# A delta-rule attention with its feed-forward on one core: the feed-forward of one chunk placed between the pieces of the next chunk's units, and two vector operations fewer in the conversion of a weight part

## The chip, the cores and the metric

The kernel runs on one core of a Trainium2 chip. The metric is the device time of one execution in microseconds (us). A core has five engines that each execute their own queue in order: TensorE (PE; its weight loads are shown apart as PEld), VectorE (DVE), ScalarE (ACT), GpSimd (POOL) and SyncE (SP), which here only issues DMAs. ScalarE issues DMAs too (the weights). Matmul results go to PSUM; everything else is in SBUF or, for two small re-layouts, in DRAM.

## The reference

For 4 batches x 8 heads, a sequence of 768 steps with a state of 48 x 48 per head, and then a feed-forward layer over all 3072 tokens with 384 features and 2048 hidden ones:

```python
k_n = k / (np.linalg.norm(k, axis=-1, keepdims=True) + 1e-06)
for t in range(S):
    y[:, :, t] = np.einsum('bhd,bhde->bhe', q[:, :, t], state)
    v_old = np.einsum('bhde,bhd->bhe', state, kt)
    state = state + bt[:, :, :, None] * np.einsum('bhd,bhe->bhde', kt, vt - v_old)
...
x = y.transpose(0, 2, 1, 3).reshape(B * S, H * D)
h = x @ w_in
g = h * (1.0 / (1.0 + np.exp(-1.702 * h)))
return (g @ w_out).astype(np.float32)
```

q, k, v and beta are fp32. The two weight matrices are fp64 and are turned into fp32 on the chip.

## The kernel before, in words

The sequence is cut into 6 chunks of 128 steps (`NC`). Within a chunk the recurrence is solved in closed form: with N the strictly lower part of beta k k^T, the updates U follow from the inverse of (1 + N), and the state is only read and written once a chunk. A *unit* is one batch in one chunk, with its 8 heads; there are 24 units.

- **Loads.** `load(n)` (lines 80 to 88) issues K, Q and V of a unit on SyncE. K has 3 buffers, V 6, Q two zero-padded tiles `QP`. Two units are loaded ahead.
- **Preparation.** `prepare(n)` (172 to 231): GpSimd and VectorE compute 1/|k| (`ksq`, `ssq`, `rn`) and the scaled `KN`; PE transposes K and Q (`psT`, line 193), ScalarE copies them to `kqT`; PE forms k k^T and k q^T (`psG`, line 205); VectorE turns the first into `Nn` (line 210), ScalarE the second into `M` (line 214), which GpSimd masks (line 216). The 32 x 32 diagonal blocks of `Nn` go through DRAM (`Nd`, four DMAs) into `NT`, where one partition holds one block of all units of the chunk.
- **Inversion.** `invert(c)` (234 to 291) inverts these 128 blocks together on VectorE: 15 steps of a product and a sum (lines 259 and 263), then eight pairs of larger ones (242 and 243), with one copy on ScalarE (267). The products `P` use the tag `gT`. The result `YB` goes back through DRAM (`Yb`), one DMA for each batch.
- **Assembly.** `assemble(n)` (294 to 359) builds the inverse of the 128 x 128 matrix from its diagonal blocks: DMAs bring the blocks into `XT` (line 304, three buffers) and `XO` (311, two buffers); then a chain of four groups of products with something between each: `ps1` (325), a copy to `P1` on VectorE (327), `ps2` (330), four activations into `XT` (335), `ps3` (349), a copy to `P3` (353), `ps4` (356), an activation (359). `L32`, `XE` and `XA` have one buffer each.
- **Step.** `advance(n, xT)` (362 to 416): `psK` (369) and two VectorE operations on V, `psU` (377), its copy `U` (381), `psS` for the state (386), `psY` (394 and 399), `x` on ScalarE (404), the state's update (409), transposes `psXT` (415) and their copy into `xT` (416), which collects two batches.
- **Feed-forward.** `feed_forward(c, b0, xT)` (419 to 444) handles two batches of a chunk: 48 products into `ph` (428), a gelu for every second hidden block into `gT` (432, tag `gT` with 5 buffers, four of which hold one half of the feed-forward), then 32 products into `po` (438), a copy and a store. A chunk has two such halves.
- **Weights.** `load_weights(part)` (151 to 165), 28 parts: a DMA on ScalarE's queue brings the fp64 words (`raw`, tag `gT`), and `from_double` (122 to 145) makes fp32 of them with seven VectorE operations.

The order: `prepare_chunk(0)` with the inversion, then for each chunk: assemble and advance its four units, in chunk 0 load the weights, prepare the next chunk and invert it, and then the chunk's feed-forward (lines 446 to 468). The program is written in this order, and a scheduler that runs when the kernel is built sets the order on each engine from it: an operation that stands earlier in the program goes first, and a later one takes its place where it is expected to be ready while the earlier ones are not. Each engine then executes its queue in that fixed order. Buffers of one tag are handed out in the order of the program.

## Time and profile before

| | before |
|---|---|
| median of 3 runs | 1281.66 us (1278.46 to 1283.55) |
| the profiled execution's own time | 1283.35 us |
| its span, first to last instruction | 1281.6 us |
| mean granted clock of TensorE | 0.768 |
| busy, PE / PEld | 1024.0 / 837.8 us |
| busy, DVE / ACT / POOL | 438.9 / 203.5 / 117.0 us |
| mean DMA rate | 36 GB/s, 46.54 MB |

A row of a view names the line of the kernel, the engine, the operation and what it writes and reads (buffer numbers left out), then busy time and mean time, or start and time taken. The trace records an fp32 product as two matmuls (48 first products of a half of the feed-forward appear as x96), a transpose as one. "<-" names what ended the idle time ahead of an instruction. "PEclk" is the clock granted to TensorE, 1.00 or 0.50 here in any one moment, and a mean over the stretch where a stretch is shown.

### The profile page before, as it was taken

The numbers are of one execution on the slowest core, as the hardware profiler recorded it, in microseconds if no ns is written. First come the engines' busy times: TensorE is split into PE (matmuls) and PEld (weight loads), VectorE is DVE, ScalarE is ACT, GpSimd is POOL, SyncE is SP. The second block draws the span as 40 slices with busy tenths as digits, with TensorE's granted clock in tenths as the row PEclk, the third lists the DMA queues.
The fourth block names the chain that finished last, engine by engine and source line by source line (L and its number), as shares of the span: only waits on it lengthen the run. The fifth ranks groups of instructions, "written<-read, shape, count | busy, mean of one in ns | idle before, by whom it ended". The sixth has DMA issues, their size and how long they took to land. (4 is left out here: it accounts for less than half of the span.)

```text
span 1281.6 us, 12617 instructions
## 1 busy us (share of the span) xinstructions
PE 1024.0 (80%) x4974; PEld 837.8 (65%) x4974; DVE 438.9 (34%) x1020; ACT 203.5 (16%) x488; POOL 117.0 (9%) x112
## 2 busy tenths in 40 slices
PE   2408971199999299999389999479999669999998
PEld 1308951077798177698267699357699457699875
DVE  4395489910233620133530132540132460022000
ACT  1202121011112111111311111311111310111100
POOL 7300013000012100022100021100010100000000
PEclk9855665599758689857789857779956879955799
DMA  6233155010102210011210011210010210000000
GB/s 101 58 110 76 47 147 139 25 39 7 33 14 39 44 40 7 19 27 31 52 33 13 16 30 29 55 34 12 15 19 1 46 33 13 15 7 1 1 13 13
DMA packets 150827, 46.54 MB, mean 36 GB/s; under 512 B 142544, under 2 KB 145616, under 8 KB 150768
## 3 DMA queue, kind: packets, MB, share of 16 engines
q1 hardware_dynamic: 146688, 33.06, 13.0%
q10 hardware_dynamic: 4080, 12.68, 3.2%
q8 instruction: 39, 0.64, 0.2%
q14 instruction: 20, 0.16, 0.0%
HBM read 34.70 MB, written 11.01 MB: 36 GB/s over the span
## 5 line engine op out<-in xcount | busy, mean ns | idle before, releaser
L428 PE MATMUL ph<-xT,w_in 128*128 128x256 f32 x1152 | 284.6, 406 | 142.6 <-ACT gT L432 142.6
L428 PEld LDWEIGHTS ph<-xT,w_in 128*128 128x128 f32 x1152 | 230.9, 205 | 178.5 <-ACT gT L432 144.9
L438 PE MATMUL po<-w_out,gT 128*128 128x384 f32 x768 | 249.6, 486 | 0.0
L438 PEld LDWEIGHTS po<-w_out,gT 128*128 128x128 f32 x768 | 145.9, 190 | 99.2
L443 DVE COPY o<-po 128x384 f32<-128x384 f32 x24 | 13.4, 557 | 413.2 <-PE po L438 413.2
L432 ACT ACTIVATE gT<-ph 128x512 f32<-128x512 f32 x96 | 56.8, 597 | 335.6 <-PE ph L428 310.3
L186 POOL TENSOR_TENSOR KN<-K,rn 128x384 f32<-128x384 f32 x24 | 20.0, 834 | 732.0 <-PE psS L386 727.4
L377 PEld LDWEIGHTS psU<-V,XT 128*128 128x128 f32 x384 | 77.2, 304 | 1.6
L377 PE MATMUL psU<-V,XT 128*128 128x48 f32 x384 | 78.0, 383 | 0.0
L325 PE MATMUL ps<-XO,L 128*128 128x32 f32 x192 | 41.2, 375 | 42.1 <-DMA XO<-Yb 42.1
L205 PE MATMUL psG<-kqT 48*128 48x256 f32 x384 | 62.9, 458 | 10.2 <-ACT kqT L194 8.0
L325 PEld LDWEIGHTS ps<-XO,L 128*128 128x128 f32 x192 | 39.1, 299 | 45.9 <-issue 42.5
L399 PE MATMUL psY<-U,M 128*128 128x48 f32 x384 | 68.9, 352 | 0.0
L399 PEld LDWEIGHTS psY<-U,M 128*128 128x128 f32 x384 | 68.3, 274 | 0.2
L205 PEld LDWEIGHTS psG<-kqT 48*128 48x128 f32 x384 | 42.9, 221 | 23.1 <-ACT kqT L194 13.3
L319 ACT ACTIVATE L<-Nn 32x128 f32<-32x128 f32 x96 | 29.5, 307 | 146.3 <-PE ps L325 144.7
L349 PE MATMUL ps<-XT,Nn 64*64 64x64 f32 x384 | 45.1, 293 | 5.6 <-ACT XT L335 5.6
L210 DVE TENSOR_TENSOR Nn<-psG,betaT 128x256 f32<-128x256 f32 x96 | 36.8, 417 | 33.5 <-PE psG L205 31.2
L356 PEld LDWEIGHTS ps<-P,XA 64*64 64x64 f32 x384 | 38.9, 202 | 13.8 <-DVE P L353 6.5
L356 PE MATMUL ps<-P,XA 64*64 64x64 f32 x384 | 43.6, 295 | 5.4 <-DVE P L353 5.4
L193 PE MATMUL psT<-ident,KN 128*128 128x128 f32 x96 | 18.5, 325 | 35.9 <-POOL KN L186 23.1
L214 ACT ACTIVATE M<-psG 128x256 f32<-128x256 f32 x96 | 34.4, 381 | 77.7 <-DVE Nn L210 68.0
(72 smaller groups left out, 983.4 us busy)
## 6 DMA issues: line engine op xcount, KB each, us to landing
raw<-in_moe_w_in_dram ACTq DMA_DIRECT2D x12, 512.0 KB, 4.4
raw<-in_moe_w_out_dram ACTq DMA_DIRECT2D x16, 384.0 KB, 3.1
K<-in_k_dram SPq DMA_DIRECT2D x24, 192.0 KB, 2.7
V<-in_v_dram SPq DMA_DIRECT2D x24, 192.0 KB, 2.8
QP<-in_q_dram SPq DMA_DIRECT2D x24, 192.0 KB, 3.1
out_dram<-o SPq DMA_DIRECT2D x24, 192.0 KB, 1.9
Nd<-Nn SPq DMA_DIRECT2D x96, 32.0 KB, 1.7
NT<-Nd SPq DMA_DIRECT2D x24, 128.0 KB, 2.4
```

The costliest lines, as they stand in the source:

```text
L205: nc.tensor.matmul(ps[hh][:, i], lhsT=kqT[pr, g + i, 0, :], rhs=kqT[pr, g + i, :, :], start=True, stop=True,)
L210: nc.vector.tensor_tensor(Nn[:, hh, g : g + 2, :], ps[hh][:, :, 0, :], bhg[:, hh, g : g + 2].broadcast_to([128, 2, 128]), op=ALU.mult,)
L214: nc.scalar.activation(M[:, hh, g : g + 2, :], ps[hh][:, :, 1, :], ACT.Copy)
L319: nc.scalar.activation(l32[o, :, o], Nn[od, hh, :, ev], ACT.Copy)
L325: nc.tensor.matmul(ps1[:, g], lhsT=l32[:, g, :], rhs=XO[:, g, :], start=True, stop=True)
L349: nc.tensor.matmul(ps3[:, h, :], lhsT=Nf[hi, h, lo], rhs=flat[hi, h, hi], start=True, stop=True)
L356: nc.tensor.matmul(ps4[:, h, :], lhsT=xa[:, h, :], rhs=P3[:, h, :], start=True, stop=True)
L377: nc.tensor.matmul(psU[:, h, :], lhsT=xt[:, h % 2, h // 2, :], rhs=V[:, h, :], start=True, stop=True)
L399: nc.tensor.matmul(psY[:, h, :], lhsT=M[:, h % 2, h // 2, :], rhs=U[:, h, :], start=(c == 0 and h == 0), stop=True, skip_group_check=True,)
L428: nc.tensor.matmul(ph[:, u], lhsT=w_in[:, j, f * 128 : (f + 1) * 128], rhs=xT[:, j, :], start=(j == 0), stop=(j == KC - 1),)
L432: nc.scalar.activation(g[:, i : i + 2, :], ph, ACT.Gelu_apprx_sigmoid)
L438: nc.tensor.matmul(po, lhsT=gT[f // FQ][:, f % FQ, i * C : (i + 1) * C], rhs=w_out[:, f, :], start=(f == 0), stop=(f == FC - 1),)
```

## The change

The functions become generators that yield at the places between pieces, with a number that is the estimated PE time of the piece. `weave(main, fill, ratio)` runs the main generator and after each of its pieces draws so many pieces of `fill` that their numbers add up to `ratio` times those of the main one. The main one, `chunk(c, xTs)`, goes through the four units of chunk c: assemble, advance, and right behind it prepare the same batch of chunk c+1 and load the unit two further on. `fill` is the weights in chunk 0 (ratio 0.5) and the feed-forward of chunk c-1 in the others (0.9, and 2.0 in the last). Behind a chunk come the inversion for the next one and what is left of `fill`. The last chunk's feed-forward runs by itself.

```diff
+    def weave(main, fill, ratio):
+        done = 0.0
+        for cost in main:
+            done += cost * ratio
+            while done > 0:
+                done -= next(fill, 1e9)
...
+    def chunk(c, xTs):
         for b in range(B):
             n = c * B + b
-            prepare(n)
-            if n + 2 < len(units):
-                load(n + 2)
-        invert(c)
-
-    prepare_chunk(0)
+            if b % HB == 0:
+                xTs.append(wk.tile([128, KC, NTH], F32, tag="xT", name="xT", bufs=3))
+            yield from assemble(n)
+            yield from advance(n, xTs[-1])
+            if c + 1 < NC:
+                yield from prepare(n + B)
+                if n + B + 2 < len(units):
+                    load(n + B + 2)
+
+    fill = weights()
+    for b in range(B):
+        run(prepare(b))
+        load(b + 2)
...
+    invert(0)
     for c in range(NC):
         xTs = []
-        for b in range(B):
-            if b % HB == 0:
-                xTs.append(wk.tile([128, KC, NTH], F32, tag="xT", name="xT"))
-            assemble(c * B + b)
-            advance(c * B + b, xTs[-1])
-        if c == 0:
-            for part in range(n_parts):
-                load_weights(part)
+        weave(chunk(c, xTs), fill, 0.5 if c == 0 else 0.9 if c + 1 < NC else 2.0)
         if c + 1 < NC:
-            prepare_chunk(c + 1)
-        for i in range(B // HB):
-            feed_forward(c, i * HB, xTs[i])
+            invert(c + 1)
+        run(fill)
+        ffn = [feed_forward(c, i * HB, xTs[i]) for i in range(B // HB)]
+        fill = (cost for work in ffn for cost in work)
+    run(fill)
```

The yields stand behind each transposed copy in the preparation, behind psG, behind ps1, ps2, ps3 and the end of the assembly, behind psK, psU, psY and the transposes of the step; in the feed-forward behind each hidden block (three products) and behind every second product into `po`. GpSimd's clearing of `YB`, `XT`, `L32`, `XE`, `XA` and `S_bd` moves from the program's start to behind chunk 0's preparation.

In the conversion of a part, two VectorE operations are replaced by one activation:

```diff
+    low = cpool.tile([128, 1], F32, name="low")
+    nc.gpsimd.memset(low, -896.0 * (1 << 23))
...
         ts(p, hi, 0x7FF * E1, None, op0=AND)
-        ts(p, p, -896.0 * E1, 0.0, op0=ALU.add, op1=ALU.max)
-        ts(p, p, 255.0 * E1, 8.0, op0=ALU.min, op1=ALU.mult)
+        nc.scalar.activation(p, p, ACT.Relu, scale=8.0, bias=low)
```

The buffers:

```diff
-        K = io.tile([128, H, D], F32, tag="K", name="K", bufs=3)
+        K = io.tile([128, H, D], F32, tag="K", name="K", bufs=2)
-    bt = cpool.tile([NBH, S], F32, name="bt")
+    bt = wk.tile([NBH, S], F32, tag="P", name="bt")
-            P = wk.tile([128, ny, nx, nk], F32, tag="gT", name="P", bufs=5)
+            P = wk.tile([128, ny, nx, nk], F32, tag="P", name="P")
-        x = wk.tile([128, DM], F32, tag="x", name="x")
+        x = wk.tile([128, DM], F32, tag="x", name="x", bufs=1)
```

(a tag without a number has two buffers; `xT` goes from two to three).

What it does to the engines' orders is seen at three places. The lines of the changed kernel are 1 to 8 lower than those of before in the preparation, the assembly and the step (psT 185, psG 198, ps1 319, ps2 325, ps3 345, ps4 353, psK 367, psU 376), ph is line 430 and po 440. First, TensorE between the end of chunk 2's preparation and chunk 2's first assembly, before:

```order
L428 MATMUL ph<-xT,w_in 128x256 x36
L438 MATMUL po<-w_out,gT 128x384 x32
L428 MATMUL ph<-xT,w_in 128x256 x48
L438 MATMUL po<-w_out,gT 128x384 x32
L325 MATMUL ps_2563<-XO,L_85 128x32 x4
L330 MATMUL ps_2570<-P_2568,XE_86 128x32 x4
L349 MATMUL ps_2582<-XT_84,Nn 64x64 x8
L356 MATMUL ps_2593<-P_2591,XA_87 64x64 x8
```

and now, from the last psG of chunk 2's preparation to chunk 2's first ps1:

```order
L198 MATMUL psG<-kqT 128x256 x7
L440 MATMUL po<-w_out,gT 128x384 x26
L430 MATMUL ph<-xT,w_in 128x256 x9
L367 MATMUL psK<-S_bd,kqT 128x96 x4
L430 MATMUL ph<-xT,w_in 128x256 x39
L440 MATMUL po<-w_out,gT 128x384 x10
L319 MATMUL ps_2321<-XO,L_85 128x32 x4
```

Before, all but twelve first products of chunk 1's feed-forward stood here; now it is the end of chunk 0's and a part of chunk 1's, and the rest of chunk 1's is spread over chunk 2.

Second, TensorE in the second unit of chunk 1, now; before, the same pieces stood with those of the neighbouring unit between them and with no feed-forward in the first two units:

```order
L319 MATMUL ps_1596<-XO,L_85 128x32 x4
L367 MATMUL psK<-S_bd,kqT 128x96 x4
L325 MATMUL ps_1606<-P_1604,XE_86 128x32 x4
L430 MATMUL ph<-xT,w_in 128x256 x2
L345 MATMUL ps_1618<-XT_84,Nn 64x64 x8
L430 MATMUL ph<-xT,w_in 128x256 x2
L353 MATMUL ps_1635<-P_1633,XA_87 64x64 x8
L185 MATMUL psT<-ident,KN_79 128x128 x4
L185 MATMUL psT<-ident,QP_81 128x128 x2
L376 MATMUL psU<-V,XT_84 128x48 x8
L185 MATMUL psT<-ident,QP_81 128x128 x2
L430 MATMUL ph<-xT,w_in 128x256 x2
```

Two products of chunk 0's feed-forward stand at each of three places in the chain, and transposes for chunk 2 beside psU.

Third, VectorE at the start of the first inversion, before:

```order
L210 TENSOR_TENSOR Nn<-psG,betaT 128x256 x12
L259 TENSOR_TENSOR P<-NT,YB 128x2
L263 TENSOR_REDUCE YB<-P 128x2
L259 TENSOR_TENSOR P<-NT,YB 128x8
L263 TENSOR_REDUCE YB<-P 128x2x2
L259 TENSOR_TENSOR P<-NT,YB 128x18
```

and now (raw, tmp and w_in belong to the conversion of the weights):

```order
L253 TENSOR_TENSOR P<-NT,YB 128x2
L176 TENSOR_SCALAR rn<-rn 128x8
L257 TENSOR_REDUCE YB<-P 128x2
L177 RECIPROCAL rn<-rn 128x8
L253 TENSOR_TENSOR P<-NT,YB 128x8
L136 SCALAR_TENSOR_TENSOR tmp<-raw,tmp 128x512
L257 TENSOR_REDUCE YB<-P 128x2x2
L137 SCALAR_TENSOR_TENSOR w_in<-w_in,tmp 128x512
L253 TENSOR_TENSOR P<-NT,YB 128x18
L132 TENSOR_SCALAR tmp<-raw 128x512
L257 TENSOR_REDUCE YB<-P 128x2x3
L134 TENSOR_SCALAR tmp<-raw 128x512
```

The conversion's first nine parts are through by then and further ones stand between the inversion's steps; before, none stood ahead of the inversion's end.

More of the change, by code (lines that the diff above doesn't have):

```diff
@@ L101 @@
     nc.gpsimd.memset(half, 0.5)
-    for t in XT + L32 + XE + XA:
-        nc.gpsimd.memset(t, 0.0)
-    nc.gpsimd.memset(YB, 0.0)
-    nc.gpsimd.affine_select(
-        out=YB, in_=YB, compare_op=ALU.not_equal, fill=1.0, base=0,
-        pattern=[[1, BS], [-1, BS]], channel_multiplier=0,
-    )
-    S_bd = cpool.tile([128, B, NP, 2, D], F32, name="S_bd")
-    nc.gpsimd.memset(S_bd, 0.0)
     psB = ps_seq.tile([128, NC, NBH], F32, tag="seq", name="psB")
@@ L257, in invert @@
         for i in range(1, HS):
[L258 removed]
+            P = wk.tile([128, 2, i, i], F32, tag="P", name="P")
             tt(
@@ L416, in advance @@
         nc.vector.tensor_copy(xT[:, :, b % HB * C : (b % HB + 1) * C], psX)
+        yield 0.5
     def feed_forward(c, b0, xT):
         gT = []
[L421 to L433 removed]
+        for f0 in range(0, FC, 2):
+            if f0 % FQ == 0:
+                gT.append(wk.tile([128, FQ, NTH], F32, tag="gT", name="gT", bufs=GB))
+            ph = ps_moe.tile([128, 2, NTH], F32, tag="moe", name="ph")
+            for u in range(2):
+                f = f0 + u
+                for j in range(KC):
+                    nc.tensor.matmul(
+                        ph[:, u], lhsT=w_in[:, j, f * 128 : (f + 1) * 128], rhs=xT[:, j, :],
+                        start=(j == 0), stop=(j == KC - 1),
+                    )
+                yield 1.3
+            nc.scalar.activation(gT[-1][:, f0 % FQ : f0 % FQ + 2], ph, ACT.Gelu_apprx_sigmoid)
         for i in range(HB):
```

48 lines of the change are left out of this document (31 added, 17 removed).

## The prediction

> **What bounds the kernel now.** I read the page first, then what waits for what, then the clock by stage, then single stretches. The page gives TensorE (PE) most of the span:
>
> ```profile
> span 1281.6 us, 12617 instructions
> PE 1024.0 (80%) x4974; PEld 837.8 (65%) x4974; DVE 438.9 (34%) x1020; ACT 203.5 (16%) x488; POOL 117.0 (9%) x112
> ```
>
> 80% busy says little by itself, because the same work runs at two speeds. The view by stretches (PE, weight loads, vector, scalar and GpSimd busy, then the granted clock) shows the start, a stretch of feed-forward alone, the assembly of chunk 1, and that chunk's last units with the preparation behind them:
>
> ```profile
> 0.00:59.09 59.09, 21.78 (x102) 15.68 (x102) 22.83 (x50) 12.58 (x29) 34.33 (x40) 0.97 0.53 86
> 288.00:320.00 32.00, 32.00 (x133) 24.88 (x132) 0.56 (x1) 4.78 (x8) 0.00 (x0) 1.00 0.02 7
> 335.56:393.60 58.04, 56.89 (x294) 53.67 (x294) 18.20 (x46) 8.98 (x28) 6.58 (x6) 0.50 0.12 22
> 393.60:427.70 34.10, 29.30 (x241) 24.79 (x239) 13.47 (x34) 12.43 (x31) 10.94 (x10) 1.00 0.34 64
> ```
>
> Feed-forward alone runs at clock 1.00. The assembly stretch occupies PE for 56.9 of its 58.0 us, but at 0.50: its products stream 32 to 96 columns each and mostly wait on weight loads (53.7 us). When wider products come among them (fourth row) the clock is 1.00 again. So there are two losses: narrow chain work at half clock, and PE without work. The waits (total, times, longest) and PE's timeline show the second; the waits' other row is used further down:
>
> ```profile
> PE ph L428 <- ACT gT L432: 142.6, 5, 45.4
> ...
> DVE rn L184 <- POOL rn L183: 53.9, 22, 5.1
> ...
> 94.47 1.89 PE L325 MATMUL ps<-XO,L 128*128 128x32 f32 x8 [42.13 <-DMA XO<-Yb]
> ```
>
> Feed-forward's third hidden tile waits five times some 28.5 us, because its buffer has the tag of the inversion's products and comes free only when the inversion ends. And no assembly starts before 94.5 us.
>
> **The price of a product at full clock.** From the chain of waits, one half of a chunk's feed-forward (48 first and 32 second products; the trace records each fp32 product twice):
>
> ```profile
> 880.93 20.72 PE ph L428 x96
> 901.65 20.64 PE po L438 x64
> ```
>
> That is 0.432 us for a first product and 0.645 for a second, 41.4 us a half. The chain's products at full clock, from PE's timeline in the fourth stretch and just ahead of it (start, time taken; the latter includes a drain of about 0.1 that the next one covers):
>
> ```profile
> 390.33 2.05 PE L428 MATMUL ph<-xT,w_in 128*128 128x256 f32 x4
> ...
> 396.44 0.79 PE L349 MATMUL ps<-XT,Nn 64*64 64x64 f32 x10
> ...
> 397.92 0.56 PE L349 MATMUL ps<-XT,Nn 64*64 64x64 f32 x6
> 398.41 1.13 PE L369 MATMUL psK<-S_bd,kqT 128*128 128x96 f32 x8
> 399.38 0.62 PE L428 MATMUL ph<-xT,w_in 128*128 128x256 f32 x2
> 399.93 1.14 PE L356 MATMUL ps<-P,XA 64*64 64x64 f32 x16
> 401.00 0.66 PE L193 MATMUL psT<-ident,KN 128*128 128x128 f32 x4
> ...
> 401.75 1.99 PE L377 MATMUL psU<-V,XT 128*128 128x48 f32 x16
> ...
> 403.81 1.03 PE L428 MATMUL ph<-xT,w_in 128*128 128x256 f32 x4
> 404.68 1.03 PE L386 MATMUL psS<-U,KN 128*128 128x96 f32 x8
> 405.54 1.06 PE L394 MATMUL psY<-S_bd,kqT 128*128 128x96 f32 x8
> 406.44 1.91 PE L399 MATMUL psY<-U,M 128*128 128x48 f32 x16
> 408.28 0.70 PE L205 MATMUL psG<-kqT 48*128 48x256 f32 x4
> 409.31 0.52 PE L415 MATMUL psXT<-ident,x 128*128 128x128 f32 x3 [0.33 <-DVE S_bd L409]
> 409.76 1.57 PE L205 MATMUL psG<-kqT 48*128 48x256 f32 x12
> ...
> 422.62 2.00 PE L205 MATMUL psG<-kqT 48*128 48x256 f32 x16 [0.37 <-ACT kqT L194]
> ```
>
> By starts: ps3 (L349) 1.28, psK 0.97, ps4 (L356) 1.07, eight transposes 1.0, psU 1.8, psS 0.86, psY 0.90 and 1.84, psXT 0.45, psG 2.27. With ps1 and ps2 (1.8, in the fence on hand-offs below) a unit, that is a batch's assembly, step and the preparation of the same batch one chunk on, costs PE **14.25 us**; in the last chunk, without psS, psG and the transposes, 10.1; in chunk 0, without psK and the state part of psY, 12.4. At half clock all double.
>
> **The change part by part.** *Weaving.* PE's order now has two kinds of stretch. Behind a chunk's last psG stands a block of feed-forward alone (28 first, 32 second and 25 first products for chunk 1: 12.1 + 20.6 + 10.8 = 43.5 us; the others come to the same). The rest stands one to six products at a time between the pieces of the units. The block has to cover the inversion, which took, after the last psG above ended at 424.6:
>
> ```profile
> 431.49 0.16 DVE L259 TENSOR_TENSOR P<-NT,YB 128x2 f32<-128x2 f32 x1 [6.08 <-DMA NT<-Nd]
> 452.30 2.07 DVE L243 TENSOR_REDUCE YB<-P 128x64 f32<-128x768 f32 x2
> 458.12 0.61 DVE L320 STREAM_TRANSPOSE XE<-XT 32x128 f32<-32x128 f32 x2 [3.75 <-DMA XT<-Yb]
> ```
>
> The way to DRAM and back ended at 431.5, the inversion at 454.4, the first blocks were back at 458.1, XO four SyncE issues of 0.47 us (row below) later: 35.5 us. The block is 8 us longer, so the 142.6 us of waiting go and nothing is late next. Two new queueings cost nothing while this holds: a copy of o stands within the inversion's vector operations (in chunks 3 to 5 its product ends 21 x 0.432 + 16 x 0.645 = 19.4 us into the block; the copy, three quarters through the inversion, is reached at 6.9 + 17 = 24), and two stores of the output stand ahead of Yb on SyncE's queue (about 1 us of the 8).
>
> *Hand-offs.* Between ps1, ps2, ps3 and ps4 PE needs a copy or an activation. Their bare price, where nothing stood between:
>
> ```profile
> 332.57 0.97 PE L325 MATMUL ps<-XO,L 128*128 128x32 f32 x8
> 333.93 1.08 PE L330 MATMUL ps<-P,XE 128*128 128x32 f32 x8 [0.39 <-DVE P L327]
> 335.93 1.96 PE L349 MATMUL ps<-XT,Nn 64*64 64x64 f32 x16 [0.93 <-ACT XT L335]
> 338.68 1.96 PE L356 MATMUL ps<-P,XA 64*64 64x64 f32 x16 [0.78 <-DVE P L353]
> ```
>
> 0.39, 0.93 and 0.78 us of idle time. Two woven first products cover 0.86: the first is hidden, the second nearly, the third too unless the vector queue is late. It can be, since V's two operations and two transposes now stand ahead of that copy. Nine units are thin (6 to 9 woven products: all of chunk 1, three of chunk 2, the first of chunks 3 and 4); I take 1.2 us each there and 0.5 in the other eleven of chunks 1 to 5: **16 us**, between 0 and 72 (three hand-offs and about as much again behind psU and psY, 3.6 us, uncovered in all twenty).
>
> *Clock.* In thin units half of the PE time is still narrow. The fourth stretch above, of a similar mix, kept 1.00 for 34 us. The opposite bound is all nine at half clock, 9 x (14.25 + 3.3) = 158 us. I take **25**, nearer the row that shows the mix. [...]
>
> *Weights.* The conversion of 28 parts moves from between chunk 0 and its feed-forward into the start and chunk 0. Rows of its two dropped operations, of an activation of the width of the one that comes in, and the timeline of one part:
>
> ```profile
> L142 DVE TENSOR_SCALAR tmp<-tmp 128x384 int32<-128x384 int32 (+1 forms) x28 | 12.0, 428 | 0.2
> L143 DVE TENSOR_SCALAR tmp<-tmp 128x384 int32<-128x384 int32 (+1 forms) x28 | 11.6, 413 | 0.3
> ...
> L432 ACT ACTIVATE gT<-ph 128x512 f32<-128x512 f32 x96 | 56.8, 597 | 335.6 <-PE ph L428 310.3 <-DVE A L243 25.3
> ...
> 81.89 0.41 DVE L139 TENSOR_SCALAR tmp<-raw 128x512 int32<-128x512 int32 x1
> ...
> 85.41 0.42 DVE L139 TENSOR_SCALAR tmp<-raw 128x512 int32<-128x512 int32 x1
> ```
>
> VectorE loses 28 x (0.428 + 0.413) = 23.5 us; ScalarE gains 28 of at most 0.6, 17 us, while it is 84% idle. A part of w_in took 3.52, now 2.7, one of w_out (384 for 512 columns) 2.0, as an estimate. The new Relu makes VectorE's next operation on that part wait for ScalarE; behind it stand Nn and the chain's copies, and behind the Relu kqT and M. Twelve parts of w_in and five of w_out now precede the first transpose of the assembly: 12 x 2.7 + 5 x 2.0 = 42 us. VectorE was idle 36 of the first 59 us (first stretch), in waits such as the 53.9 / 22 = 2.5 us each for GpSimd's power. If the parts fill all of it, the start is later by 42 - 36 = 6; if none, by 42. GpSimd's clearing of the large tiles now follows the first K; it can only help, and I count nothing for it. I take **13 later: 107.5 us**, near the full end of the fit, since five parts stand within the inversion, where VectorE has no gap.
>
> *Chunk 0.* Its first two units have no feed-forward between them: half clock, 2 x 24.8, plus 5 each for hand-offs that eleven parts of w_out on VectorE now delay. The other two have 20 woven products (8.6) and warm up on the way: 2 x 12.4 + 8.6 + 10 of cold remainder and hand-offs. Together **103** (58 if all is at full clock and covered; 4 x 24.8 + 17 + 20 = 136 if all is at half clock and no hand-off covered). After it, at 210.5, feed-forward goes on at once, where it now waits for the weights and the second inversion.
>
> *Queues and buffers.* Each unit sends SyncE 17 issues (three loads, four Nd, NT, four XT, four XO, one store) of about 0.47 us:
>
> ```profile
> 426.27 1.41 SPq L226 DMA_DIRECT2D Nd<-Nn  x3
> ```
>
> 8 us of a unit of 18 or more. Loads that wait for K's, Q's or V's buffer hold back XT and XO behind them, but with three XT buffers these go out two units ahead, which hides it; without that cover PE would wait the row's 1.4 us in a unit, inside the 72. P, K, x, xT and bt change buffers only; P's own tag is what frees gT.
>
> **The sum**, in span: start 107.5 + chunk 0 103 + feed-forward left 12 x 41.36 - 8.6 = 487.7 + units 16 x 14.25 + 4 x 10.1 = 268.4 + hand-offs 16 + clock 25 + last copy and store 3 = 1010.6. The profiled execution took 1283.35 us for its span of 1281.6, so 1.75 lie around it, and it is 0.1% above the median of 1281.66. **Forecast 1012 us.**
>
> **Rivals.** (a) *Full clock all through*: the clock term is 0, **987**. For it: the fourth stretch. Against: it has more psG than a thin unit.
>
> (b) *Every thin unit falls to half clock*, in its 4.6 us from ps4 over the transposes to the end of psU, and does not recover within it: +158 - 25, **1145**. For it: the third stretch stayed at 0.50 though it was occupied. Against: in the fourth, the same ps4, transposes and psU (399.9 to 403.8) passed at 1.00. [...]
>
> (c) *The fixed queues cost what the weave gains*: hand-offs at 72 and the start at its late end (+29): 1012 + 56 + 29 = **1097**. For it: VectorE's order mixes three kinds of work. Against: nearly every hand-off has products behind it.
>
> (d) *Slower*: the woven work keeps the half clock throughout, feed-forward's pieces included. Woven feed-forward is 487.7 - 5 x 43.5 - 82.7 (the last chunk's own) = 187.5; with the units' 268.4 that doubles 456 us: 987 + 456 = **1443**. It decides from 296 of these 456 at half clock, where the time is the 1283 of before. For it: the third stretch stayed at 0.50 although single first products stand in it too. Against: two first products in a row (390.33) sufficed to open it at 393.6, and thin units have such pairs.
>
> (e) *It does not do what it says*: the builder sets the order by itself and may have woven as far as data allow. Then 1282. Against: the block ahead of each inversion's end and the pieces between ps1 to ps4 stand in the new order.
>
> **Chances.** Forecast 0.64, (a) 0.15, (b) 0.07, (c) 0.10, (d) 0.03, (e) 0.01. The range runs from 954 (start 100, chunk 0 85, hand-offs 8, clock 0: 952 + 2) to 1091 (start and chunk 0 120 each, hand-offs 40, clock 50: 1089 + 2), and leaves out (b), (d), (e) and half of (c), 0.16. About 0.5% is what a measurement here can tell from no change: faster 0.96, same 0.01, slower 0.03.
>
> **What would show it.** Right: the wait of ph for gT gone; units of chunks 1 and 2 of about 18.5 us at clock near 1; chunks 1 to 4 some 140 to 155 us apart; first ps1 near 107 and the block behind chunk 0 near 210; PE idle under 5% from there. Wrong: ps1 before 98 or after 120, thin units over 25 us, PE waiting for XO at the end of a block, or the clock at 0.50 for whole units in chunks 3 to 5.

## The result, and the profile after

The changed kernel takes 999.9 us (median of 4 runs, 991.46 to 1004.89) against 1282.49 us before: 0.779 of the time, 95% interval 0.773 to 0.786. The profiled execution took 1003.42 us for a span of 1001.7 us. Some executions of the kernels below are disturbed as a whole, over 1.5% above the fastest of their kernel: the ratios leave those out (two of six are left for wide products in chunk 0), so it is the ratios that are compared, while the profiles of ratio 0 with two wide products (1036.6 us) and of chunk 0 opened (1028.1 us) are of disturbed executions.

The page of after: its head, the granted clock in 40 slices, and the group of first products (busy, mean ns, idle time ahead):

```profile
span 1001.7 us, 12586 instructions
PE 900.5 (90%) x4974; PEld 707.8 (71%) x4974; DVE 417.7 (42%) x964; ACT 222.2 (22%) x516; POOL 116.6 (12%) x113
...
PEclk9999999999789998899997999995999999999999
...
L430 PE MATMUL ph<-xT,w_in 128*128 128x256 f32 x1152 | 280.6, 394 | 0.0
```

The same 4974 matmul records now occupy PE for 900.5 us instead of 1024.0. Nothing of the work went away, so these 123.5 us of the gain are put down to a faster clock: in the traces 402 us of PE's busy time lie under a recorded 0.50 before, and 65 us after, besides what chunk 0 has ahead of the point where the record of after begins (see below). The rest is PE's idle time: 101 us of 1001.7 where it was 258 of 1281.6.

The view by stretches: the start, chunk 0 up to its feed-forward, that block, chunk 1 up to its block, and all from behind chunk 2's third unit on (the columns are those of the same view before):

```profile
0.00:107.55 107.55, 23.70 (x103) 17.19 (x103) 88.84 (x188) 24.94 (x48) 36.92 (x40) 1.00 0.55 137
107.55:199.50 91.95, 86.57 (x509) 73.90 (x509) 48.84 (x124) 32.38 (x78) 14.90 (x14) 1.00 0.35 80
199.50:243.05 43.55, 43.55 (x173) 32.34 (x172) 27.72 (x60) 6.06 (x11) 2.88 (x3) 1.00 0.17 35
243.05:326.37 83.32, 80.31 (x575) 67.54 (x574) 29.28 (x76) 25.34 (x66) 15.01 (x15) 0.90 0.23 44
...
438.06:1001.70 563.64, 557.17 (x3020) 434.62 (x3019) 172.65 (x397) 110.56 (x258) 33.74 (x31) 0.97 0.12 26
```

The block behind chunk 0 is 43.55 us without a hole, as long as predicted. One trap: the record of the clock begins with its first change, at 169.0 us here, and the view writes 1.00 ahead of it. Chunk 0 nevertheless ran at half clock: its first unit, 26.3 us with PE busy for 23.2, takes 26.6 with 23.25 in the run with two wide products below, which changes nothing in chunk 0 and whose record begins earlier and says 0.50 there:

```profile
106.07:132.64 26.57, 23.25 (x116) 20.07 (x116) 14.76 (x37) 7.58 (x18) 1.65 (x2) 0.50 0.42 97
```

So mean clocks of whole runs are not compared here.

What PE waits for (total, times, longest):

```profile
PE ps L319 <- DMA XO<-Yb: 58.1, 1, 58.1
...
PE ps L325 <- DVE P L322: 7.9, 6, 1.5
```

ph's wait for gT (142.6 us before) is not among them, and the group of first products above has 0.0 in its last column. The one long wait left is that for the first XO. The next in this list that belongs to the units is ps2's wait for P1, 7.9 us. Small as it is, it marks the place where the clock is lost. PE's timeline of the second unit of chunk 1:

```profile
260.71 1.08 PE L319 MATMUL ps<-XO,L 128*128 128x32 f32 x8
261.62 1.11 PE L367 MATMUL psK<-S_bd,kqT 128*128 128x96 f32 x8
263.96 1.37 PE L325 MATMUL ps<-P,XE 128*128 128x32 f32 x8 [1.23 <-DVE P L322]
265.15 2.05 PE L430 MATMUL ph<-xT,w_in 128*128 128x256 f32 x4
267.13 1.97 PE L345 MATMUL ps<-XT,Nn 64*64 64x64 f32 x16
...
274.26 3.49 PE L376 MATMUL psU<-V,XT 128*128 128x48 f32 x16
```

ps1 and psK still take their full-clock times; from the end of ps2 on all takes nearly twice as long (psU 3.49 us instead of 1.99). The granted clock went to 0.50 at 264.5 us and came back at 281.6. It does this five times after chunk 0, in the second unit of chunks 1, 3 and 4 and in the second and third of chunk 2: 64.9 us at half clock, so some 32 us lost, since PE is busy all through. Each time the 3.4 us ahead of the fall hold PE's wait between ps1 and ps2 (1.2 to 1.5 us). Two such units carry 17 woven products; the first units of chunks 1 to 4 carry 7 to 9, have feed-forward between ps1 and ps2, and keep the clock.

### The profile page after: what moved, and what is told of

It reads as the page before. It is cut to its first block, busy times and chain, and to the rows that moved or that the text cites. A ratio compares the mean times of both kernels' runs of the same rounds, so it can differ in the third digit from the quotient of the medians.

```text
span 1001.7 us, 12586 instructions
## 1 busy us (share of the span) xinstructions
PE 900.5 (90%) x4974; PEld 707.8 (71%) x4974; DVE 417.7 (42%) x964; ACT 222.2 (22%) x516; POOL 116.6 (12%) x113
## 4 chain that ended last, share of the span: by engine, by line
PE 81%; DVE 7%; POOL 5%; issue 3%; DMA 3%; ACT 1%; ACTq 0%; POOLq 0%
PE ph L430 26%; PE po L440 26%; PE psU L376 5%; PE psY L399 3%; PE psG L198 3%; PE ps L353 3%; PE ps L345 3%; PE ps L325 2%; POOL rn L175 2%; PE psT L185 2%; PE psS L386 2%; DMA K<-in_k_dram 2%; PE ps L319 2%; PE psK L367 1%; PE psY L394 1%
## 5 line engine op out<-in xcount | busy, mean ns | idle before, releaser
L440 PE MATMUL po<-w_out,gT 128*128 128x384 f32 x768 | 269.0, 500 | 0.0
L319 PE MATMUL ps<-XO,L 128*128 128x32 f32 x192 | 27.0, 287 | 58.1 <-DMA XO<-Yb 58.1
L319 PEld LDWEIGHTS ps<-XO,L 128*128 128x128 f32 x192 | 26.7, 208 | 65.1 <-issue 60.4
L376 PEld LDWEIGHTS psU<-V,XT 128*128 128x128 f32 x384 | 52.7, 217 | 4.8 <-issue 2.9
L447 DVE COPY o<-po 128x384 f32<-128x384 f32 x24 | 13.3, 555 | 102.3 <-PE po L440 102.3
L376 PE MATMUL psU<-V,XT 128*128 128x48 f32 x384 | 53.2, 298 | 0.0
L399 PE MATMUL psY<-U,M 128*128 128x48 f32 x384 | 49.1, 284 | 0.0
L399 PEld LDWEIGHTS psY<-U,M 128*128 128x128 f32 x384 | 48.2, 204 | 0.1
L175 POOL TENSOR_TENSOR rn<-ssq,half 128x8 f32<-128x8 f32 x24 | 40.0, 1668 | 47.0 <-DVE ssq L173 40.6
L186 ACT ACTIVATE kqT<-psT 128x512 f32<-128x512 f32 x48 | 26.8, 595 | 76.4 <-PE psY L394 49.7
L314 DVE STREAM_TRANSPOSE XE<-XT 32x128 f32<-32x128 f32 x96 | 28.8, 300 | 33.2 <-PE ps L325 28.0
L253 DVE TENSOR_TENSOR P<-NT,YB 128x2 f32<-128x2 f32 (+14 forms) x90 | 29.7, 330 | 24.2 <-DMA NT<-Nd 21.7
```

Of the source, the lines that this page charges most:

```text
L175: nc.gpsimd.tensor_tensor(rn, ssq, half, op=ALU.pow)
L319: nc.tensor.matmul(ps1[:, g], lhsT=l32[:, g, :], rhs=XO[:, g, :], start=True, stop=True)
L376: nc.tensor.matmul(psU[:, h, :], lhsT=xt[:, h % 2, h // 2, :], rhs=V[:, h, :], start=True, stop=True)
L399: nc.tensor.matmul(psY[:, h, :], lhsT=M[:, h % 2, h // 2, :], rhs=U[:, h, :], start=(c == 0 and h == 0), stop=True, skip_group_check=True,)
L440: nc.tensor.matmul(po, lhsT=gT[f // FQ][:, f % FQ, i * C : (i + 1) * C], rhs=w_out[:, f, :], start=(f == 0), stop=(f == FC - 1),)
```

## The experiments

Time and ratio against the kernel before, from the runs of one comparison; the last column is the time at half clock in the one profiled execution, in falls that begin after 230 us, without its very end. Where two intervals overlap, the order of the two kernels is not shown.

| run | ratio (95% interval) | at before's 1282.5 us | half clock, us |
|---|---|---|---|
| after | 0.779 (0.773 to 0.786) | 999.6 | 65 |
| tag alone | 0.889 (0.886 to 0.892) | 1140.5 | 311 |
| ratio 0 | 0.792 (0.789 to 0.795) | 1015.5 | 82 |
| seven operations | 0.798 (0.795 to 0.801) | 1023.7 | 85 |
| shared tag | 0.861 (0.856 to 0.865) | 1103.8 | 99 |
| two wide products | 0.789 (0.787 to 0.792) | 1012.4 | 79 |
| four narrow products | 0.772 (0.770 to 0.775) | 990.3 | 55 |
| ratio 0, two wide | 0.799 (0.795 to 0.803) | 1024.3 | 79 |
| wide in chunk 0 | 0.781 (0.778 to 0.785) | 1002.0 | 48 |
| five wide products | 0.764 (0.761 to 0.766) | 979.6 | 0 |
| chunk 0 opened | 0.789 (0.786 to 0.791) | 1011.6 | 55 |
| ratio 0.6 | 0.769 (0.766 to 0.771) | 985.9 | 27 |
| chunk 0 opened, five wide | 0.774 (0.771 to 0.777) | 992.8 | 0 |

**The tag alone.** The theory: the change is worth the wait for gT (by the tag) plus the clock in the units (by the weaving). Rivals: one of the two is all.

```diff
-            P = wk.tile([128, ny, nx, nk], F32, tag="gT", name="P", bufs=5)
+            P = wk.tile([128, ny, nx, nk], F32, tag="P", name="P")
```

> The kernel before with nothing changed but the tag: the inversion's products P get a tag of their own, and K, x and bt give up buffers for it as in the change. The program's order and the seven vector operations stay. Theory: the tag takes away the waits of ph for gT (142.6 us) and nothing else, since feed-forward still stands in one block and the units stay at half clock: 1283 - 143 = about 1140 us (1120 to 1160), unit after unit of chunks 1 to 5 still 25 to 29 us apart. Rival 1: the weaving is what covers the inversion, and the tag by itself buys less than 40 us: over 1240. Rival 2: the tag is all there is: within 20 us of the kernel after, below 1020.

1140 us. The start and two units of chunk 1 by stretches:

```profile
0.00:114.58 114.58, 23.67 (x103) 17.20 (x103) 102.30 (x229) 13.26 (x30) 39.71 (x39) 1.00 0.54 132
...
302.15:322.73 20.58, 20.58 (x109) 19.63 (x108) 6.32 (x15) 3.38 (x10) 1.66 (x2) 0.50 0.17 29
322.73:344.21 21.48, 21.48 (x110) 20.06 (x109) 7.61 (x19) 3.38 (x10) 4.84 (x4) 0.50 0.10 19
```

The wait is gone and the units stay at 0.50, as the theory has it. They follow each other by 20.6 and 21.5 us, as they do before the change, and not by the 25 to 29 that were expected. From here to after, half-clock time with PE busy falls from 311 to 65 us, which is 123 of the remaining 141 us. The first row shows something not foreseen: VectorE is 102.3 us busy ahead of the first ps1. The conversion moves into the start although its place in the program is the old one, because its buffers have the tag gT and are free as soon as P leaves it.

**The ratios.**

```diff
-        weave(chunk(c, xTs), fill, 0.5 if c == 0 else 0.9 if c + 1 < NC else 2.0)
+        weave(chunk(c, xTs), fill, 0.5 if c == 0 else 0.0)
```

> The kernel after with the weave's ratio at 0 from chunk 1 on: feed-forward of chunk c-1 is written behind chunk c and the inversion, in one piece. The builder then still puts 5 to 9 feed-forward products into each unit by itself, where the kernel after has 6 to 9 in nine units and 12 to 47 in the other eleven. Theory: the clock falls in thin units with an uncovered hand-off between ps1 and ps2; there are now up to twenty thin units instead of nine, so five to eleven more of them fall, at 6 to 7 us each: 1030 to 1080 us. Rival 1: without the ratios the units fall to half clock altogether as before the change, twenty times about 14 us less what falls already: over 1200. Rival 2: the ratios do nothing that the builder does not do: 1000 within 6 us.

1015 us: between the theory and rival 2, nearer the latter. The clock falls six times from chunk 1 on and not ten or more as the theory had it. Written behind the next chunk, feed-forward is taken into the units by the builder itself; the ratios add 16 us, and 17 us less at half clock account for 8.5 of it.

**The Relu.**

```diff
-        nc.scalar.activation(p, p, ACT.Relu, scale=8.0, bias=low)
+        ts(p, p, -896.0 * E1, 0.0, op0=ALU.add, op1=ALU.max)
+        ts(p, p, 255.0 * E1, 8.0, op0=ALU.min, op1=ALU.mult)
```

> The kernel after with the two vector operations of each weight part back in place of the Relu on ScalarE. VectorE gets 28 x (0.428 + 0.413) = 23.5 us more, in the start and in chunk 0. Theory: 17 of the 28 parts stand ahead of the first assembly, where VectorE is 88.8 us busy of 107.6; the 14 us of these come through for the most part, and some of chunk 0's 9 us: first ps1 at 114 to 121, time 1008 to 1022 us. Rival: the gaps take it all, first ps1 within 3 us of 107.6 and the time within 6 us of 1000.

24 us slower, just above the theory's range, and not by its path: the first ps1 is where the rival has it. The first ps1 of this run and its start by stretches:

```profile
109.92 1.46 PE L320 MATMUL ps<-XO,L 128*128 128x32 f32 x6 [58.31 <-DMA XO<-Yb]
```

```profile
0.00:109.92 109.92, 23.70 (x102) 17.20 (x103) 100.35 (x218) 13.22 (x30) 40.76 (x40) 1.00 0.54 134
```

The first ps1 is only 2.4 us later; VectorE's gaps take 11.5 us more work (100.35 against 88.84). Chunk 1 begins 9.5 us later than after's (252.6 against 243.05), so 7 us came in chunk 0. The two profiled executions differ by 18.8 us; the other 9 come later, where the program is the same: 20 us more at half clock, 10 of the time. That part need not be a price of the two operations: it hangs on where the clock falls, for which see the rule below.

**The tag back, the weaving kept.**

```diff
-            P = wk.tile([128, ny, nx, nk], F32, tag="P", name="P")
+            P = wk.tile([128, ny, nx, nk], F32, tag="gT", name="P", bufs=GB)
```

> The kernel after with the inversion's products P back in the tag gT with five buffers; the weaving stays. The builder then puts only 32 products into the first inversion's block and some 80 into the others, and more (22 to 33) into the later units of each chunk. Theory: ph waits for gT again behind each of the five inversions, less what the woven pieces have done by then: 15 to 25 us each, 75 to 125 in all: 1075 to 1125 us. Rival: a block of 80 products (34 us or more) covers the inversion's 35 us without a fresh gT, and the thicker units keep the clock at 1.00: 975 to 1005 us.

1104 us, as the theory said: the waits first, then the start and a unit of chunk 2:

```profile
PE ph L430 <- ACT gT L435: 121.8, 5, 35.8
```

```profile
0.00:91.02 91.02, 23.92 (x102) 17.05 (x103) 53.17 (x120) 15.82 (x34) 34.24 (x40) 1.00 0.44 92
408.31:435.57 27.26, 27.26 (x191) 24.02 (x190) 8.31 (x21) 8.66 (x21) 3.35 (x4) 1.00 0.19 38
```

The weaving without the tag gives back 122 us of waits. Four of its five falls of the clock lie in these waits (23.9 us from 361.6 on, with PE busy for 6 of them), so its 99 us in the table are mostly not lost by the clock; one unit of chunks 1 to 5 falls. The conversion is pushed behind the inversion (VectorE 53 us busy in the start), and the first ps1 comes at 91.0: with 107.55, 109.9 and 114.6 above, the start does depend on what VectorE converts there. The thicker unit, 33 products, keeps 1.00.

**What takes the clock away.** The theory at this point: the hole between ps1 and ps2 does it, and wide products in it would hold the clock. Two were put there in the seven units that had the hole:

```diff
+        if n in (5, 6, 7, 9, 10, 13, 17):
+            for _ in range(2):
+                nc.tensor.matmul(
+                    pw[:, NP:], lhsT=w_in[:, 0, 0:128],
+                    rhs=w_in[:, 0, 0:256].rearrange("p (g i) -> p g i", i=BS),
+                    start=True, stop=True,
+                )
```

> The kernel after, with two products of 256 columns (of w_in with itself, into a part of the ps2 tile that nobody reads) placed between ps1 and ps2 in the seven units of chunks 1 to 4 in which PE stood idle there for 0.7 to 1.5 us. They add 7 x 0.86 = 6 us of work and compute nothing that is used. Theory: the clock falls because this stretch (ps1, psK, idle, ps2) streams too little, so with wide products in it the five falls go (64.9 us at half clock, about 32 us lost) and the time is 965 to 982 us with the clock at 1.00 in chunks 1 to 4. Rival 1: the hole is only idle time and the clock falls for another reason: falls stay, 995 to 1010. Rival 2: the falls move to the next narrow stretch (ps4, transposes, psU), 985 to 1000.

The theory failed: 1012 us, slower than after. The clock falls six times, in six of the seven units that got the products. The same unit as above:

```profile
257.62 1.08 PE L319 MATMUL ps<-XO,L 128*128 128x32 f32 x8
258.53 1.11 PE L327 MATMUL ps<-w_in 128*128 128x256 f32 x4
260.78 1.08 PE L333 MATMUL ps<-P,XE 128*128 128x32 f32 x8 [1.14 <-DVE P L322]
261.69 1.11 PE L375 MATMUL psK<-S_bd,kqT 128*128 128x96 f32 x8
263.12 1.97 PE L353 MATMUL ps<-XT,Nn 64*64 64x64 f32 x16 [0.32 <-ACT XT L339]
```

The two products took psK's place; psK slid behind ps2, the hole stayed at 1.14 us, and the clock fell ahead of ps3 (262.7 us). In the same comparison, four products of 32 columns in that place:

```diff
-            for _ in range(2):
+            for g in range(4):
                 nc.tensor.matmul(
-                    pw[:, NP:], lhsT=w_in[:, 0, 0:128],
-                    rhs=w_in[:, 0, 0:256].rearrange("p (g i) -> p g i", i=BS),
-                    start=True, stop=True,
+                    pw[:, NP + g], lhsT=w_in[:, 0, g * 128 : (g + 1) * 128],
+                    rhs=w_in[:, 0, 0:BS], start=True, stop=True,
                 )
```

> As the run with two wide products, but with four products of 32 columns in their place, which keep PE occupied for as long (ps1 has four of this kind and takes 0.97 us) and stream hardly anything. Theory (what counts is streamed columns): the clock still falls in the same units or in more of them, 998 to 1020 us. Rival (what counts is that PE is occupied): as with the wide products, 965 to 982 us.

990 us, between the two theories and better than the wide ones, which neither has. The same place in the same unit:

```profile
258.12 1.06 PE L327 MATMUL ps<-w_in 128*128 128x32 f32 x8
259.02 0.66 PE L374 MATMUL psK<-S_bd,kqT 128*128 128x96 f32 x4
260.37 1.08 PE L332 MATMUL ps<-P,XE 128*128 128x32 f32 x8 [0.69 <-DVE P L322]
```

Here half of psK stayed in the hole, the idle time fell to 0.69, and the clock still fell five times, but came back sooner. The interval overlaps after's, and why this run is better than the one with two wide products is not shown.

With the ratios at 0 and two wide products in all twenty units:

```diff
+        if c > 0:
+            for _ in range(2):
...
```

> The kernel after with the ratio at 0 from chunk 1 on (1015.3 us by itself, mean clock 0.90) and two wide products between ps1 and ps2 in each of the twenty units of chunks 1 to 5. Theory: what the ratios were worth is the clock of thin units, so with the falls gone the time drops below that of the kernel after, although 20 x 0.86 = 17 us of work come in, of which the holes take 10: 970 to 990 us. Rival: the ratios also cover hand-offs that the wide products don't: 1005 to 1020.

1024 us, slower than without them (1015; the two intervals just touch), and beyond even the rival. Some 17 us of work came in, and the time at half clock stayed as it was, 79 us against 82.

Eight wide products in each unit of chunk 0, two behind each of ps1 to ps4:

```diff
+        if n < B:
+            for _ in range(2):
...
+        warm(n, P1.rearrange("p g i -> p (g i)"), slice(0, 128))
...
+        warm(n, flat[hi, 0, hi], hi)
...
+        warm(n, P3[:, 0:2, :].rearrange("p h i -> p (h i)"), lo)
```

> The kernel after with eight wide products (of KN with the unit's own P1, XT, P3 or the identity, into tiles that nobody reads) between the pieces of each unit of chunk 0: two behind each of ps1, ps2, ps3 and ps4. They add 4 x 8 x 0.43 = 14 us of work that computes nothing used. Theory: chunk 0's first three units (26.3, 25.4, 23.1 us) run at half clock for want of wide products; at full clock their narrow work takes 12.4, the wide products 3.4, uncovered hand-offs some 3: 18 to 20 us a unit, 14 to 20 us less in all: 980 to 988. Rival 1: the conversion on VectorE sets their pace (it is 14 us busy in each): no gain, 995 to 1010. Rival 2: the added work costs what the clock gives: 992 to 1000.

1002 us, no gain. Its first two units, 28.8 and 26.8 us, are longer than after's 26.3 and 25.4: rival 1 by its number, but not by its reason, since PE and not VectorE is busy all through (28.77 of 28.77 us in the first) and the clock does not open before 155.5 us.

**A rule from the traces.** All changes of the clock lie on a grid of 3.41 us in each profile (in after those at 264.53, 281.60 and 394.24 us are 5 and 33 steps apart). I cut the profiles into these steps and added up for each what PE streams: a product's columns times its rows out of 128, at 1.69 ns a column (0.432 us for 256), half of that for a transpose, which is recorded once and not twice. In the unit of after shown above, the step from 261.12 to 264.53 holds psK, 4 x 96 columns, 0.65 us, and ten records of ps1 and ps2, 0.25: 0.90 of 3.41, or 0.26. The step behind it runs at 0.50. Over the 14 profiles of this case, 3797 steps, some 690 of them with half clock in the step behind, one threshold sorts all but 7: **behind a step with 0.37 of a full-clock step or more the clock was full, behind one with less it was half.** The 7 lie between 0.366 and 0.394. The second digit hangs on how a record that crosses a cut is divided: in proportion to its time, the best threshold is 0.38, with four to seven exceptions. The rule was formed on ten of the profiles; the four taken later add some 1050 steps, of which two to four are exceptions. Without the weight by rows the best threshold leaves 110 wrong, with PE's occupied time instead 490. (The expectations below say 0.365: transposes were counted at half of this then, with 15 exceptions.) So the failures read plainly. Ahead of the falls, two wide products left steps of 0.30 to 0.36, the narrow ones 0.24 to 0.32. In chunk 0, where half clock halves what can be streamed (two first products take 2.05 us instead of 1.03), no step of the first unit and a half exceeded 0.35 with eight wide products a unit.

By the same rule it matters where the cuts between steps fall, and no run here controls that. In after, the last unit of chunk 1 has the same hand-off as the second, with nearly the same wait:

```profile
309.56 1.05 PE L325 MATMUL ps<-P,XE 128*128 128x32 f32 x8 [1.09 <-ACT L L313]
```

A cut at 308.9 us divides this wait, the steps on both sides come to 0.39 and 0.49, and the clock stays. The second units of chunks 3 and 4 hold the same products and take 29.9 and 34.8 us. One fall in after is 7 to 20 us at half clock, so as an estimate this alone can make a difference of 3 to 10 us between kernels in which the waits remain.

The rule was then tried on the same seven units, with five wide products instead of two:

```diff
-            for _ in range(2):
+            for _ in range(5):
```

> As the run with two wide products between ps1 and ps2 in seven units, but with five, which fill the whole 2.2 us from the end of ps1 to the start of ps2. Ten profiles taken so far, cut into the 3.41 us steps in which the granted clock changes, suggest a rule: the clock is 1.00 in the step that follows when the columns streamed in a step, each weighted by its rows out of 128, come to at least 0.365 of what a step can stream at full clock, and 0.50 when they don't. The steps that lost it hold ps1, psK, an idle wait and ps2 (0.26 in the kernel after, 0.31 to 0.35 with two wide products). Five wide products bring every such step above 0.38. Theory (this rule): no falls in those seven units, some 32 us less than the kernel after for at most 3 us of added PE time: 966 to 980 us. Rival (wide products do not hold the clock here, as with two): 1005 to 1030.

980 us, at the upper end of what the rule's theory has. The unit's hand-off on PE's timeline, then three units by stretches:

```profile
257.45 1.08 PE L319 MATMUL ps<-XO,L 128*128 128x32 f32 x8
258.36 2.40 PE L327 MATMUL ps<-w_in 128*128 128x256 f32 x10
260.61 1.08 PE L333 MATMUL ps<-P,XE 128*128 128x32 f32 x8
261.52 1.11 PE L375 MATMUL psK<-S_bd,kqT 128*128 128x96 f32 x8
```

```profile
239.78:257.45 17.67, 17.67 (x143) 15.10 (x141) 6.43 (x16) 6.08 (x16) 1.66 (x2) 1.00 0.27 55
257.45:277.38 19.93, 19.62 (x155) 16.92 (x154) 8.53 (x23) 6.44 (x18) 4.38 (x4) 1.00 0.26 49
655.73:681.84 26.11, 25.78 (x176) 20.89 (x176) 8.96 (x24) 7.76 (x21) 3.60 (x4) 1.00 0.15 28
```

27.0 and 34.8 us in after are now 19.9 and 26.1. From 165 us on no step is below 0.43, and the clock stays at 1.00 to the end. By itself this run doesn't tell streaming from occupied time, since the five products also close the wait; the count over all steps does, and before's assembly, which was occupied for 56.9 of 58.0 us at 0.50.

Chunk 0 with more wide products and an opening ahead of its first ps1:

```diff
+        if n == 0:
...
+            for u in range(8):
+                nc.tensor.matmul(pd[:, u % 2], lhsT=ident, rhs=full[:, 0:NTH], start=True, stop=True)
...
-            for _ in range(2):
+            for _ in range(5):
```

> As the run with wide products in chunk 0, but with five instead of two behind ps1, and with eight more (of the first unit's XT, into a tile that nobody reads) right ahead of the first ps1, to open the clock before chunk 0 begins: at half clock a step needs 0.365 of full capacity, which is 73 percent of its time in wide products, and no step of chunk 0 had over 0.34 with two of them at a place. Work that computes nothing used: 52 products, 22 us at full clock. Theory (the rule of 0.365): chunk 0 runs at full clock from its start, units of 17 to 20 us instead of 26, 25, 23 and 17, first ps1 2 to 5 us later: 980 to 995 us. Rival 1: chunk 0's first steps at half clock have another cause, and the added products come on top: 1015 to 1035. Rival 2: VectorE's conversion sets the pace, 1000 to 1010.

1012 us, slower than after, and between the two rivals' ranges. In its profile the clock opened at 108.1, 138.8 and 169.6 us and fell at 118.4, 145.7 and 176.4, behind steps of 0.37, 0.31 and 0.38 with ps4 in each; the first and the last of these are at the rule's edge, which does not decide them. The added products there have 64 rows and count half. In the last run they have 128 behind ps3, and the five wide products of chunks 1 to 4 are in:

```diff
-        warm(n, flat[hi, 0, hi], hi)
+        warm(n, 2, flat[:, 0, :], slice(0, 128))
...
+        warm(n, 2, U[:, 0:2, :].rearrange("p h d -> p (h d)"), slice(0, 128))
```

> The run with five wide products in seven units (978.7 us), and chunk 0 filled so that by the rule of 0.365 no step after its opening falls below it: eight wide products (of the first unit's XT) ahead of the first ps1, and in each of its four units four behind ps1, two behind ps2, two behind ps3 with all 128 rows (the earlier run had 64 there, which count half), three of 64 rows behind ps4 and two behind psY, where a step would otherwise hold the tail of psY, an idle wait for x, psXT and little else. They write tiles that nobody reads: 60 products, 26 us at full clock. Theory (the rule): chunk 0 keeps the full clock, units of 18 to 21 us instead of 26.4, 25.5 and 21.0; because the added products cost most of what the clock gives, only 3 to 12 us less than without: 966 to 976 us. Rival: chunk 0 falls to half clock again for a reason that the rule doesn't hold: units of 25 us or more, 995 to 1025 us.

993 us: neither. Chunk 0's units and the last of them with its block, then two places on PE's timeline:

```profile
109.32:129.45 20.13, 18.43 (x143) 15.27 (x141) 16.78 (x43) 8.59 (x20) 0.83 (x1) 1.00 0.48 125
129.45:154.26 24.81, 22.94 (x142) 19.64 (x142) 15.98 (x41) 7.96 (x20) 4.60 (x4) 0.79 0.44 100
154.26:174.10 19.84, 18.24 (x141) 15.42 (x142) 8.15 (x22) 6.04 (x17) 4.35 (x4) 1.00 0.20 40
174.10:251.72 77.62, 75.78 (x319) 58.78 (x320) 32.75 (x75) 13.71 (x29) 7.93 (x7) 0.82 0.15 29
```

```profile
137.66 1.63 PE L382 MATMUL ps<-P,XA 64*64 64x64 f32 x16 [1.39 <-DVE P L379]
...
178.78 1.70 PE L352 MATMUL ps<-P,XE 128*128 128x32 f32 x8 [1.79 <-DVE P L334]
```

The first and third unit took 20 us, as the theory said. The clock fell twice, behind steps of 0.352 and 0.366, each with a wait for VectorE of 1.4 to 1.8 us that the plan had not allowed for, and the second fall lasted 27 us. The rule held; the cover did not, and 26 us of added products eat what the clock gives. They also displace useful ones: the 20 feed-forward products that stand in chunk 0's third and fourth unit in after and in the run with five wide products stand behind chunk 0 here (0.432 us each, 8.6 us).

**A version without added work.** Instead of useless products, the woven ones spread more evenly:

```diff
-        weave(chunk(c, xTs), fill, 0.5 if c == 0 else 0.9 if c + 1 < NC else 2.0)
+        weave(chunk(c, xTs), fill, 0.5 if c == 0 else 0.6 if c + 1 < NC else 2.0)
```

> The kernel after with the ratio of chunks 1 to 4 at 0.6 instead of 0.9. The builder then puts 9, 7, 9 products into the units of chunk 1 (as before), 7, 6, 6 into chunk 2, 9, 21, 16 into chunk 3 and 21, 21, 16 into chunk 4, and 93 to 102 into the blocks. Theory: chunk 4's first units are no longer thin, so one fall of some 10 us goes; the third of chunk 2 gets thinner: 985 to 1003 us, the difference that of half-clock time alone. Rival: a block of 93 to 102 products no longer covers the inversion and the assembly waits for XO: over 1006.

986 us. A fallen unit of chunk 1 and the first of chunk 4 (17.66 us and 9 products in after, 21 products here):

```profile
261.93:287.68 25.75, 24.27 (x147) 20.96 (x146) 8.39 (x23) 6.45 (x18) 4.38 (x4) 0.73 0.21 44
635.10:658.36 23.26, 23.26 (x174) 20.21 (x172) 8.69 (x22) 6.70 (x17) 3.29 (x3) 1.00 0.26 50
```

Three falls are left, in chunks 1 and 2, 27 us instead of 65; that is 19 us of clock, and the time shows 14. The blocks of 93 to 102 products still cover the inversion: no wait for XO. This and the five wide products are the versions whose intervals lie below after's; those of the narrow products and of chunk 0 opened with five wide overlap it. The two were not run together.

## Why the prediction was right, and where it was off

999.9 us against a forecast of 1012, inside the range of 954 to 1091. In the span that is 1001.7 for 1010.6: chunk 0 was put 11 us too long, clock and hand-offs together 2 too short. Term by term:

- **The gT wait goes, and the block covers the inversion.** Right. The two runs on the tag show it from both sides: with it and no weaving 0 us of that wait, with weaving and no tag 121.8.
- **Start, 107.5.** Measured 107.55, and the runs with 53, 89 and 100 us of VectorE work ahead of the first ps1 (91.0, 107.55, 109.9) bear out that the conversion moves it. That the number fits to the tenth is luck: 13 was chosen between 6 and 42, and kernels with the same program up to there have 105.7 to 107.55. What moved it was put too simply: the tag is what lets the conversion in, as the tag alone has 114.6 and the change without the tag 91.0.
- **Chunk 0, 103.** The mis-sized term: 92.0. I gave its first two units 29.8 us each, for hand-offs that conversion parts would delay by 5; they took 26.3 and 25.4. The third and fourth, 40.2 together, were put at 43.4. The half clock in the first two was right.
- **Units and feed-forward.** Right: 14.25 + 8 x 0.432 = 17.7 for a thin unit at full clock, and 17.66 to 18.7 measured.
- **Clock, 25, and hand-offs, 16.** Measured 32 (64.9 us at half clock) and, for what is left of 1001.7 once the other terms are taken off, some 11; together 43 for 41. That the sum fits so well is partly luck, the one 7 short and the other 5 over. That narrow stretches fall to half clock was right, and the place was wrong. I looked for the fall in thin units, with rival (b) between ps4 and psU, and for late hand-offs at P3. Both stand mostly between ps1 and ps2. Two of the five fallen units were not thin by my count, and the limit of 25 us a thin unit that I gave was broken by two thin ones, 27.0 and 26.7. What sorts the falls is how much is streamed in a 3.41 us step (0.37 of full clock, with 7 exceptions in 3797 steps), not how many products a unit has.
- **The Relu.** 23.5 us of VectorE work taken out were worth 24 us of time, more than I allowed, but only about 9.5 up to chunk 1; behind it, most of the rest is the clock falling in other steps.
- **Rivals.** (a) would have been right for the clock from chunk 1 on with the five wide products. (b) is out: three of the nine thin units fell. (c) is out: hand-offs cost some 11 us and not 72, and the start was not later than forecast. (d) and (e) are out: woven feed-forward ran at half clock only within the five falls. The ratio at 0 shows a part of (e): the builder weaves by itself once the program's order lets it.
- **The signs.** The first ps1, PE's idle time behind chunk 0 (12 of 802 us) and the thin units that kept the clock came as foretold. The block behind chunk 0 began 11 us early, and chunk 1 took 128 us from its first ps1 to chunk 2's, below the 140 to 155 that were given.

What stays open: whether the 7 steps that the rule sorts wrongly are more than an error of counting at its edge, why the threshold has this size, how much of chunk 0 could be had if its products were useful, and how much the time of each kernel varies with where the cuts fall.

## What to carry to other kernels

When a busy engine is slow, ask what it streams: a chain of narrow products with one wait of 1.2 to 1.5 us among them was followed by half clock for 7 to 20 us five times here, and what held the clock was enough wide work at that very place (five wide products: no fall; two: six falls); how many wide products a unit had in all did not decide it. A shared buffer tag orders work as firmly as the program does; here it held back feed-forward, and it also held the weight conversion in its place. Filling a hole moves what stood in it: look at where the displaced work goes before counting the gain.

## What the runs showed of the hardware

In each of the 14 profiles the granted clock changed on a grid of 3.41 us. Behind 0.37 or more of full-clock streaming in a step, weighted by rows, it was full, behind less it was half, for rising and for falling alike (7 exceptions in 3797 steps). At half clock the same amount means 74% of a step in wide products, which fits with a stretch that has lost the clock keeping it lost (7 to 20 us in after's falls). Leaving the transposes out of the sum makes the rule wrong in 101 steps instead of 7; so in these traces they do count, by their columns like any other record.
